# Attention into a mixture of experts: V's split on ScalarE and VectorE, eight weight sums on VectorE, and another order for attention

## The chip, the cores and the metric

One core of a Trainium2 chip runs the whole program in one launch. The engines are TensorE (PE for its matmuls, PEld for its weight loads), VectorE (DVE), ScalarE (ACT), GpSimd (POOL) and SyncE (SP), each with its own queue that runs in program order; engines wait for each other through semaphores. The metric is device time in microseconds (us). Before the change three runs took 1684.28, 1685.58 and 1691.61 us; their median is 1685.58 us.

## The reference

Attention over 4 batches, 8 heads, 576 positions and a head width of 64, with rotary position turns on q and k; its output is the input x (2304 tokens by 512) of a mixture of 8 experts, all of which see all tokens:

```python
q_rot, k_rot = (rotate(q), rotate(k))
scores = 1.0 / np.sqrt(D) * np.matmul(q_rot, k_rot.transpose(0, 1, 3, 2))
attn = np.exp(scores - np.max(scores, axis=-1, keepdims=True))
attn = attn / (np.sum(attn, axis=-1, keepdims=True) + 1e-09)
x = np.matmul(attn, v)                      # tokens by 512
logits = x @ w_gate                         # 8 experts
P = np.exp(logits - logits.max())
for _ in range(8):
    P /= P.sum(1, keepdims=True) + 1e-09
    P /= P.sum(0, keepdims=True) + 1e-09
    P *= N / E
for e in range(E):
    out += P[:, e:e + 1] * (np.maximum(x @ w1[e], 0.0) @ w2[e])
```

## The kernel before

**Number format.** Operands of most matmuls are split into a half-precision high part and a half-precision low part (the rest after the high part is taken away), and three products (high by high, high by low, low by high) are summed. So each operand has an instruction that makes its high part and one that makes its low part. Values are first scaled by a power of two taken from the tensor's largest magnitude.

**Attention.** The work goes by 16 pairs of heads. A pair has five score operations on TensorE (line 406, tile `s`), which make nine units of 128 queries; the third operation makes one unit, the others two. A unit passes VectorE's row maximum (line 410, `nm`), ScalarE's exponential (line 417), VectorE's reciprocal of the row sum (lines 423 and 425), ScalarE's scaled high part (line 428, `et`), VectorE's low part (line 292, `et`) and a DMA transpose from SP's queue (lines 458 and 462, `ET<-et`). When five or four units of a pair are transposed, TensorE multiplies them with V (line 477, `g<-ET,vv`, 30 matmuls for half a pair), and lines 487 and 489 write the high and low part of x (`xx`). Scores lie in three PSUM tiles, so a new score operation waits until an older unit has left its tile. In 4 units of 9 the exponential goes to SBUF (tile `e`), in the other 5 it stays in PSUM (`s`). GpSimd turns q and k of the coming pairs (lines 357 and 361, tile `raw`, six instructions a pair).

**V.** V comes a batch (four pairs) at a time. VectorE takes its largest magnitude (line 289, `vmx`, then `vm`), TensorE and VectorE spread it over the partitions (lines 660, 664, 667), VectorE makes the scale. Then each pair has three steps: `v_x` on GpSimd (line 384) multiplies V by the scale in place, `v_hi` on ScalarE (line 379) rounds it to the high part, `v_lo` on GpSimd (line 388) subtracts.

**Expert 0 as filler.** Expert 0's matmuls F1 (line 611) and F2 (line 630) fill TensorE while attention runs: F1 may begin when the first batch's x and the split of w1 are there, F2 when the split of w2 is there. That split has the same three steps as V's (lines 549, 545, 553, eight of each for w1 and for w2).

**Between attention and the experts** (from about 426 us) TensorE finishes expert 0; VectorE runs the gate's eight normalisations (lines 852 to 864), sums over blocks of x (lines 912 to 937) and the splits of the first half of expert 1's weights (line 292, `w1l` and `w2l`). The later experts use a scheme with seven products in place of eight, for which the weight quarters are added and subtracted four times per matrix; `total` (line 1042) does this on GpSimd, in place, so the order is: split three quarters, four sums, split the four sums. All weights of one matrix lie in one staging tile; the next matrix is loaded when the last split has read it.

**The order.** `Plan.run` lists every operation with an engine, an assumed duration and a due number `at`, and puts them into the engines' queues by a simulated schedule: of the operations that are ready on a free engine, the one with the lowest due number goes first. Durations are in `US`; due numbers are `AT` or `AT_NEW` (by operation, counted in units) plus a shift from `SH1`. GpSimd operations, and VectorE operations marked `lock`, are not planned at the same time. The experts' part has a plan of its own.

Of the kernel before, what the change touches and what calls it, by code (L numbers as in the profile page):

```python
# [14 lines left out]
ALU = mybir.AluOpType  # L15
# [47 lines left out]
    ld=-78.23, cq=-29.0, ck=-28.0, vx=-11.0, sq=-29.0, sk=-28.0, aq=-28.5, ak=-27.5, vh=-10.0, vl=-9.0, h0=4.69, l0=5.19,  # L63
    h1=9.69, l1=10.19, S=-20.0, M=-20.0, ex=-20.0, eh=-10.0, el=-10.0, TR=-10.0, AV=5.0, ei=-20.0,
)
AT_NEW = dict(ldv=-30.41, v0=-10.46, v1=-9.46, v2=-8.46, v3=-7.46, vg=-6.96, vr=-6.86, vp=-6.46)
AV_AT = ((3, 0, 0), (3, 0, 1), (4, 0, 2), (5, 0, 3), (6, 0, 4), (7, 1, 0), (8, 1, 1), (9, 1, 2), (10, 1, 3), (11, 1, 4))

SH1 = dict(
    cq=11.55, sq=11.55, aq=11.55, el=9.37, vh=-16.21, ld=10.14, M=-76.45, S=-26.64, eh=-9.66, ex=-20.25, ck=-11.34,  # L70
    sk=-11.34, ak=-11.34, ldv=-6.42, AV=-36.11, TR=10.32, vx=11.72, vl=-32.41, x0=1.13, h0=1.13, l0=1.13, x1=1.13,
    h1=1.13, l1=1.13, ei=-12.59,
)

US = dict(
# [147 lines left out]
def attention_moe(ctx, tc, qk, v, trigs, eye, wg, w1, w2, out):  # L223
# [67 lines left out]
    def stt_lo(lo, x, s, hi):  # L291
        dve.scalar_tensor_tensor(lo, x, s, hi, op0=ALU.mult, op1=ALU.subtract)  # L292
# [82 lines left out]
    def v_hi(p):  # L375
        t = att.tile([P, 2, 640], F16, tag="vv", bufs=NVV, name="vv")
        vhl[p] = [t[:, n].rearrange("p (j a d) -> p j a d", j=2, a=5) for n in range(2)]
        b, c = divmod(p, KC)
        act.copy(vhl[p][0], vraw[b][:, c])

    def v_x(p, e):
        b, c = divmod(p, KC)
        x = vraw[b][:, c].rearrange("p j a d -> p (j a d)")
        engine[e].tensor_scalar(x, x, vs[b], None, op0=ALU.mult)

    def v_lo(p, e):
        b, c = divmod(p, KC)
        engine[e].tensor_tensor(vhl[p][1], vraw[b][:, c], vhl[p][0], op=ALU.subtract)

    HEADS = [slice(0, 64), slice(64, P)]  # L390
    QH = [slice(0, HS), slice(HS, S)]
# [258 lines left out]
    def choice(pool_us, dve_us):  # L650
        return (("pool", US[pool_us]), ("none", 0.0))[:1] + ((("dve", US[dve_us]),) if BOTH else ())
# [25 lines left out]
    def pair_ops(p):  # L677
# [4 lines left out]
        def add(k, e, us, fn, deps=(), **kw):  # L682
            e = e if isinstance(e, tuple) else (e, US[us])
            plan.add(f"{k}.{p}", e, at[k], fn, [d if "." in d else f"{d}.{p}" for d in deps], **kw)
# [11 lines left out]
        for i in range(5):  # L696
# [14 lines left out]
            for j in range(1 if i == TAIL else 2):  # L711
# [19 lines left out]
                    f"TR.{m}", ("sp", US["TR"]), at["TR"] + u + off(u), lambda m=m: e_turn(m), [f"el.{m}"] + [f"et{h}.{p}" for h in hs],  # L731
                    uses=[e] + [(f"ET{h}", p) for h in hs], allocs=tails if u == 4 else [],
                )
        add("vx", choice("tsv", "tsd"), 0, lambda e: v_x(p, e), [f"vp.{b}"], uses=[("vraw", b)])
        add("vh", "act", "vh", lambda: v_hi(p), ["vx"], allocs=[("vhl", p)], uses=[("vraw", b)])
        add("vl", choice("plv", "tt"), 0, lambda e: v_lo(p, e), ["vh"], uses=[("vraw", b), ("vhl", p)])
        done = None
        for s, qh, jt in AV_AT:
            a, et = ("G", ("av", p, qh)), (f"ET{qh}", p)
# [63 lines left out]
    def w0_ops():  # L803
        plan.add("gx", ("dve", 0.3), 8, gate_max)
        last, g = top_ops("g", 8, "gx", lambda: w0m["g"])
        plan.add("gs", ("dve", 1.0), 8, gate_scale, [last], uses=[g], lock=True)
        for n, at in ((1, 16.95), (2, 66.94)):
            r = ("raw0", n)
            for i in range(4):
                plan.add(  # L810
# [147 lines left out]
    def w_part(plan, q, n, w, at, gap, last):  # L958
# [3 lines left out]
        def put(k, eng, us, fn, deps, **kw):  # L962
            nonlocal at
            at += gap
            plan.add(f"{k}.{n}.{q}", (eng, us), at + (SH2.get(k[0:2], 0.0) if q else 0.0), fn, [x if "." in x else f"{x}.{n}.{q}" for x in deps], **kw)
# [57 lines left out]
        def quad(a, d=d, n=n):  # L1023
            if n == 1:
                x = d["r"].rearrange("p (c h f) -> p c h f", c=KC, h=2)
                return {"11": x[:, 0:2, 0], "12": x[:, 2:4, 0], "21": x[:, 0:2, 1], "22": x[:, 2:4, 1]}[a]
            x = d["r"].rearrange("p (h c e f) -> p h c e f", h=2, c=2, e=2)
            return x[:, int(a[0]) - 1, :, int(a[1]) - 1]
# [10 lines left out]
            put(f"wl{i}", "dve", US["wl"], lambda: lo(i, a), [f"wh{i}"], uses=[raw], lock=True)  # L1039

        def total(k, o, x, y, op, deps):
            put(k, "pool", US["ptt"], lambda: pool.tensor_tensor(quad(o), quad(x), quad(y), op=op), deps, uses=[raw])  # L1042

        if n == 1:
            split(A22, "22")
# [378 lines left out]
```

## Time and profile before

| what | us |
|---|---|
| median of three runs | 1685.58 |
| the profiled execution | 1691.59 |
| its span, first to last instruction | 1689.6 |
| PE busy, 13990 matmuls | 1583.7 |
| DVE busy | 1377.7 |
| ACT busy | 1054.4 |
| POOL busy | 616.1 |

The busy times are of the whole span; two thirds of it is the experts' stage, which keeps TensorE full. The page's 40 slices of 42.2 us show three stages: in the first six TensorE is busy for three to eight tenths, in the next six for nine, and then for nine to the end. The granted TensorE clock is 0.97 on the mean, and below full speed only in slices of attention. The profiled execution took 6.0 us more than the median run, so differences are worked out against it and then taken from the median.

### The profile page before, as it was taken

What the parts mean: (1) busy time and instruction counts of PE and PEld (TensorE: products, weight loads), DVE (VectorE), ACT (ScalarE), POOL (GpSimd) and SP (SyncE); (2) the same over time, 40 slices, a digit from 0 to 9 for tenths busy, and PEclk for the clock granted to TensorE, in tenths of its full rate; (3) what the DMA queues carried; (4) which work ended last, traced back from release to release, by engine and by line L of the source; (5) the groups of instructions that cost most, each with busy time, mean ns of one, the idle gap of its engine ahead of it and who ended that gap; (6) DMA issues with size and microseconds to landing.
All of it is one profiled execution on the core that took longest, in us unless ns stands there. A gap on an engine that the chain in (4) does not pass through costs nothing.

```text
span 1689.6 us, 35290 instructions
## 1 busy us (share of the span) xinstructions
PE 1583.7 (94%) x13990; PEld 1274.3 (75%) x13990; DVE 1377.7 (82%) x2736; ACT 1054.4 (62%) x2145; POOL 616.1 (36%) x504
## 2 busy tenths in 40 slices
PE   3676889999998999999999999999999999999998
PEld 2343445445456898989989898989898989898987
DVE  7667977877797888888888888888888878888877
ACT  3565766656237666666666666666666666666642
POOL 4767774620252423232323323232323323333310
PEclk9767988999999999999999999999999999999999
DMA  7899989977122565656555565655555555565532
GB/s 215 176 184 189 213 177 188 190 155 125 54 88 100 125 151 125 151 132 157 125 151 136 140 138 143 157 131 146 138 151 138 143 133 155 126 161 130 127 111 94
DMA packets 244853, 243.61 MB, mean 144 GB/s; under 512 B 195792, under 2 KB 195920, under 8 KB 241104
## 3 DMA queue, kind: packets, MB, share of 16 engines
q1 hardware_dynamic: 225968, 180.02, 39.5%
q0 software_dynamic: 18720, 61.35, 20.3%
q8 instruction: 109, 1.79, 0.4%
q14 instruction: 56, 0.46, 0.1%
HBM read 123.36 MB, written 9.44 MB: 79 GB/s over the span
## 4 chain that ended last, share of the span: by engine, by line
PE 79%; DVE 8%; DMA 3%; ACT 2%; issue 2%; SPq 0%; POOLq 0%; ACTq 0%; DVEq 0%
PE m L1092 66%; PE s L406 4%; PE g L477 4%; DMA ET<-et 3%; PE g L630 3%; PE g L611 2%; DVE et L292 2%; DVE nm L410 1%; DVE hl L621 1%; DVE ts L912 0%; ACT accA L879 0%; ACT et L428 0%; ACT e L417 0%; DVE w1l L292 0%; DVE ei L425 0%
## 5 line engine op out<-in xcount | busy, mean ns | idle before, releaser
L1092 PE MATMUL m<-w2h,h 128*128 128x256 f16 x3528 | 627.2, 273 | 3.2 <-DVE accB L1155 1.5
L1092 PEld LDWEIGHTS <-h 128*128 128x128 f16 x5292 | 515.3, 98 | 63.5 <-issue 2.0
L1092 PE MATMUL m<-w2l,h 128*128 128x256 f16 x1764 | 480.8, 273 | 0.0
L1092 PEld LDWEIGHTS <-w1h 128*128 128x128 f16 x3920 | 369.2, 98 | 39.9 <-issue 3.0
L1092 PE MATMUL m<-ts,w1h 128*128 128x256 f16 (+1 forms) x2240 | 347.6, 262 | 2.7 <-ACT m L1115 1.4
L1157 ACT ACTIVATE ev<-m,pp 128x256 f32<-128x256 f32 x468 | 197.6, 467 | 185.8 <-PE m L1092 184.8
L1092 PE MATMUL m<-ts,w1l 128*128 128x256 f16 (+1 forms) x1120 | 284.0, 262 | 0.0
L1092 PE MATMUL m<-xx,w1h 128*128 128x256 f16 (+1 forms) x1680 | 261.4, 262 | 0.0
L1042 POOL TENSOR_TENSOR wraw<-wraw 128x512 f32<-128x512 f32 x112 | 160.8, 1436 | 169.3 <-issue 140.6
L1092 PE MATMUL m<-xx,w1l 128*128 128x256 f16 (+1 forms) x840 | 213.1, 262 | 0.0
L1137 POOL TENSOR_TENSOR h<-u,h 128x512 f16<-128x512 f32 (+1 forms) x70 | 78.2, 1116 | 357.7 <-ACT h L1133 348.8
L1092 PEld LDWEIGHTS <-w1l 128*128 128x128 f16 x1960 | 191.8, 98 | 17.7
L1155 DVE SCALAR_TENSOR_TENSOR ev<-m,pp,ev 128x256 f32<-128x256 f32 x351 | 154.8, 478 | 45.4 <-ACT ev L1157 28.3
L406 PE MATMUL s<-raw 64*128 64x288 f32 (+1 forms) x640 | 136.7, 509 | 49.7 <-ACT e L417 19.5
L1133 ACT ACTIVATE h<-m 128x512 f16<-128x512 f32 (+1 forms) x210 | 120.4, 574 | 44.4 <-PE m L1092 40.8
L406 PEld LDWEIGHTS s<-raw 64*128 64x128 f32 (+1 forms) x640 | 72.2, 211 | 99.8 <-issue 28.0
L410 DVE TENSOR_REDUCE nm<-s 128x1 f32<-128x576 f32 x144 | 103.6, 752 | 48.6 <-PE s L406 48.1
L1118 DVE TENSOR_TENSOR u<-m,u 128x512 f32<-128x512 f32 (+1 forms) x140 | 88.9, 635 | 54.9 <-PE m L1092 29.2
L1133 ACT ACTIVATE h<-u 128x512 f16<-128x512 f32 (+1 forms) x210 | 122.4, 586 | 14.8 <-DVE u L1144 11.1
L1115 ACT COPY u<-m 128x512 f32<-128x512 f32 (+1 forms) x140 | 75.8, 541 | 71.5 <-PE m L1092 70.4
L1165 POOL DMA_DIRECT2D accA<-ev x78 | 69.0, 1021 | 126.5 <-ACT ev L1157 108.4
L1165 POOL DMA_DIRECT2D accB<-ev x52 | 45.1, 867 | 181.7 <-ACT h L1133 111.0
(148 smaller groups left out, 2629.8 us busy)
## 6 DMA issues: line engine op xcount, KB each, us to landing
ts<-xd SPq DMA_DIRECT2D x110, 512.0 KB, 3.8
accA<-ev POOLq DMA_DIRECT2D x78, 512.0 KB, 6.1
wraw<-in_w SPq DMA_DIRECT2D x28, 1024.0 KB, 4.9
raw<-in_qk SPq DMA_DIRECT2D x32, 576.0 KB, 5.0
accB<-ev POOLq DMA_DIRECT2D x26, 512.0 KB, 7.1
ts<-xd SPq DMA_DIRECT2D x28, 256.0 KB, 2.9
accB<-ev POOLq DMA_DIRECT2D x26, 256.0 KB, 3.3
vraw<-in_v SPq DMA_DIRECT2D x16, 320.0 KB, 4.4
```

Of the source, the lines that this page charges most:

```text
L406: pe.matmul(o, q, x[r, 1, QH[kh]], start=True, stop=True)
L410: dve.tensor_reduce(b[0], ps[:, :, 0:HS], axis=AX.XY, op=ALU.max, negate=True)
L477: pe.matmul(po[r, m : m + e.shape[-1]], x[:, j, jt, :], e[:, j, 5 * n + jt, :], start=jt == i == 0 and x is vh and n == 0, stop=jt == 4 an ...
L1042: put(k, "pool", US["ptt"], lambda: pool.tensor_tensor(quad(o), quad(x), quad(y), op=op), deps, uses=[raw])
L1092: pe.matmul(live[bank][:, f_ * width : (f_ + 1) * width], step(x, i, f_), y[:, i], start=first and f_ == 0 and n == 0, stop=n == 5, skip_g ...
L1115: act.copy(live[n], live[src])
L1118: dve.tensor_tensor(live[n], live[x], live[n], **add)
L1133: act.activation(t[:, 0:cols], live[src], func)
L1137: engine[eng].tensor_tensor(l, live[src], h, **sub)
L1155: dve.scalar_tensor_tensor(o, x, s, o, op0=ALU.mult, op1=ALU.add)
L1157: act.activation(o, x, AF.Copy, scale=s)
L1165: pool.dma_start(out=accs(th * NT2 + t0_, nt), in_=ev[th][:, 0:nt], accum_op=ALU.add)
```

## The change

V's split loses the step `v_x`: `v_hi` now scales and rounds in one ScalarE instruction (`hi_of`), and `v_lo` scales and subtracts in one VectorE instruction (`stt_lo`, a scalar_tensor_tensor on V, the scale and the high part). 32 GpSimd instructions go, 16 VectorE instructions come. In the first half-expert after expert 0 (`q == 0`) the eight sums of weight quarters go from GpSimd to VectorE. The shifts `SH1`, V's due numbers and those of expert 0's weights are other numbers, and the queues of the attention stage come out in another order. The helpers `hi_of` and `stt_lo` are those that the later experts' weights use already.

```diff
--- before.py
+++ after.py
@@ -63,13 +63,13 @@
...
 )
-AT_NEW = dict(ldv=-30.41, v0=-10.46, v1=-9.46, v2=-8.46, v3=-7.46, vg=-6.96, vr=-6.86, vp=-6.46)
+AT_NEW = dict(ldv=-30.41, v0=-13.01, v1=-12.01, v2=-11.01, v3=-10.01, vg=-9.51, vr=-9.41, vp=-9.01)
 AV_AT = ((3, 0, 0), (3, 0, 1), (4, 0, 2), (5, 0, 3), (6, 0, 4), (7, 1, 0), (8, 1, 1), (9, 1, 2), (10, 1, 3), (11, 1, 4))
 
 SH1 = dict(
-    cq=11.55, sq=11.55, aq=11.55, el=9.37, vh=-16.21, ld=10.14, M=-76.45, S=-26.64, eh=-9.66, ex=-20.25, ck=-11.34,
...
+    cq=-13.64, sq=-13.64, aq=-13.64, el=6.36, vh=-33.79, ld=6.54, M=-83.95, S=-86.81, eh=-10.31, ex=-37.95, ck=7.42,
...
 )
 
 US = dict(
@@ -376,16 +376,11 @@
         t = att.tile([P, 2, 640], F16, tag="vv", bufs=NVV, name="vv")
         vhl[p] = [t[:, n].rearrange("p (j a d) -> p j a d", j=2, a=5) for n in range(2)]
         b, c = divmod(p, KC)
-        act.copy(vhl[p][0], vraw[b][:, c])
-
-    def v_x(p, e):
+        hi_of(vhl[p][0], vraw[b][:, c], vs[b])
+
+    def v_lo(p):
         b, c = divmod(p, KC)
-        x = vraw[b][:, c].rearrange("p j a d -> p (j a d)")
-        engine[e].tensor_scalar(x, x, vs[b], None, op0=ALU.mult)
-
-    def v_lo(p, e):
-        b, c = divmod(p, KC)
-        engine[e].tensor_tensor(vhl[p][1], vraw[b][:, c], vhl[p][0], op=ALU.subtract)
+        stt_lo(vhl[p][1], vraw[b][:, c], vs[b], vhl[p][0])
 
     HEADS = [slice(0, 64), slice(64, P)]
     QH = [slice(0, HS), slice(HS, S)]
@@ -731,9 +726,8 @@
                     f"TR.{m}", ("sp", US["TR"]), at["TR"] + u + off(u), lambda m=m: e_turn(m), [f"el.{m}"] + [f"et{h}.{p}" for h in hs],
                     uses=[e] + [(f"ET{h}", p) for h in hs], allocs=tails if u == 4 else [],
                 )
-        add("vx", choice("tsv", "tsd"), 0, lambda e: v_x(p, e), [f"vp.{b}"], uses=[("vraw", b)])
-        add("vh", "act", "vh", lambda: v_hi(p), ["vx"], allocs=[("vhl", p)], uses=[("vraw", b)])
-        add("vl", choice("plv", "tt"), 0, lambda e: v_lo(p, e), ["vh"], uses=[("vraw", b), ("vhl", p)])
+        add("vh", "act", "vh", lambda: v_hi(p), [f"vp.{b}"], allocs=[("vhl", p)], uses=[("vraw", b)])
+        add("vl", "dve", "vl", lambda: v_lo(p), ["vh"], uses=[("vraw", b), ("vhl", p)], lock=True)
         done = None
         for s, qh, jt in AV_AT:
             a, et = ("G", ("av", p, qh)), (f"ET{qh}", p)
@@ -804,7 +798,7 @@
         plan.add("gx", ("dve", 0.3), 8, gate_max)
         last, g = top_ops("g", 8, "gx", lambda: w0m["g"])
         plan.add("gs", ("dve", 1.0), 8, gate_scale, [last], uses=[g], lock=True)
-        for n, at in ((1, 16.95), (2, 66.94)):
+        for n, at in ((1, 16.2), (2, 104.48)):
             r = ("raw0", n)
             for i in range(4):
                 plan.add(
@@ -1039,7 +1033,8 @@
             put(f"wl{i}", "dve", US["wl"], lambda: lo(i, a), [f"wh{i}"], uses=[raw], lock=True)
 
         def total(k, o, x, y, op, deps):
-            put(k, "pool", US["ptt"], lambda: pool.tensor_tensor(quad(o), quad(x), quad(y), op=op), deps, uses=[raw])
+            e_ = "dve" if q == 0 else "pool"
+            put(k, e_, US["tt" if q == 0 else "ptt"], lambda: engine[e_].tensor_tensor(quad(o), quad(x), quad(y), op=op), deps, uses=[raw], lock=True)
 
         if n == 1:
             split(A22, "22")
```

The first place is VectorE at the beginning, some 35 us into the run: `vm` is V's maximum for the first batch, `wgs` the gate's weights, `wmx` the maximum of expert 0's weights, `top` the step that spreads a maximum. Before:

```order
L279 TENSOR_SCALAR e<-g 128x1
L283 TENSOR_SCALAR inv<-e 128x1
L285 RECIPROCAL s<-inv 128x1
L588 TENSOR_SCALAR wgs<-wgt,s 128x4x8
L589 SCALAR_TENSOR_TENSOR wgs<-wgt,s,wgs 128x4x8
L289 TENSOR_REDUCE wmx<-wraw 128x1
L289 TENSOR_REDUCE vmx<-vraw 128x1
L328 TENSOR_REDUCE vm_299<-vmx 128x1
L289 TENSOR_REDUCE wmx<-wraw 128x1
L664 TENSOR_REDUCE top_309<-g 1x1
```

Now:

```order
L289 TENSOR_REDUCE wmx<-wraw 128x1
L289 TENSOR_REDUCE vmx<-vraw 128x1
L328 TENSOR_REDUCE vm_297<-vmx 128x1
L292 SCALAR_TENSOR_TENSOR et_99<-s,ei,et_99 128x576
L659 TENSOR_REDUCE top_311<-g 1x1
```

The gate's scale and split (lines 279 to 589 of before) stood ahead of the last part of V's maximum; now they come after the first two low parts of V, 24 rows of the order later than V's maximum. On TensorE the turn of this maximum stood with its second matmul directly ahead of the scores of the second pair; now a score operation of four matmuls lies between the two matmuls.

The second place is GpSimd from the third pair's turns on: `raw` with `trig` and `trigq` are k's and q's turns, `vraw` and `vv` V, `wraw` and `wl` expert 0's weights. Before:

```order
L357 TENSOR_TENSOR raw<-raw,trig 128x576 x2
L361 TENSOR_TENSOR raw<-raw 128x576
L357 TENSOR_TENSOR raw<-raw,trigq 128x576 x2
L384 TENSOR_SCALAR vraw<-vraw,s 128x640
L361 TENSOR_TENSOR raw<-raw 128x576
L384 TENSOR_SCALAR vraw<-vraw,s 128x640
L388 TENSOR_TENSOR vv<-vraw,vv 128x640 x2
L357 TENSOR_TENSOR raw<-raw,trig 128x576 x2
L361 TENSOR_TENSOR raw<-raw 128x576
L357 TENSOR_TENSOR raw<-raw,trigq 128x576 x2
L361 TENSOR_TENSOR raw<-raw 128x576
L384 TENSOR_SCALAR vraw<-vraw,s 128x640 x2
```

Now:

```order
L357 TENSOR_TENSOR raw<-raw,trigq 128x576 x2
L361 TENSOR_TENSOR raw<-raw 128x576
L357 TENSOR_TENSOR raw<-raw,trig 128x576 x2
L361 TENSOR_TENSOR raw<-raw 128x576
L357 TENSOR_TENSOR raw<-raw,trigq 128x576 x2
L361 TENSOR_TENSOR raw<-raw 128x576
L357 TENSOR_TENSOR raw<-raw,trig 128x576 x2
L361 TENSOR_TENSOR raw<-raw 128x576
L544 TENSOR_SCALAR wraw<-wraw,s 128x512 x2
L548 TENSOR_TENSOR wl<-wraw,wh 128x512
L544 TENSOR_SCALAR wraw<-wraw,s 128x512
```

V's steps are gone from between the turns, and expert 0's first weight split follows the turns directly. In the whole stage the last low part of w1 now stands after the turns of 5 pairs, where it stood after 6; the last of w2 after those of 10, where it stood after 9 (pair 0's turns, which `prep0` makes, are not counted). On TensorE the first F1 matmul comes after 24 of the 80 score operations and before after 28; the first F2 after 46 and before after 41. By the 46th score operation 96 of the 480 filler matmuls of attention had been placed, and before 132. F1 and F2 of the same blocks are left for after attention in both. The multiplications with V of the first two pairs come one to three score operations sooner, most others stand as far behind their scores as before.

The third place is VectorE in the stage between attention and the experts, from the last gate operation on (line 866 of before, 860 now); 1037 is `total`. Before:

```order
L866 TENSOR_TENSOR prob<-prob,ctok 128x144
L292 SCALAR_TENSOR_TENSOR w1l<-wraw,s,w1h 128x512
L925 TENSOR_TENSOR m_5083<-m_5083,c_5084 128x512
L927 TENSOR_TENSOR u_5085<-xx,m_5083 128x512
L292 SCALAR_TENSOR_TENSOR w1l<-wraw,s,w1h 128x512
L930 TENSOR_TENSOR u_5085<-u_5085,xx 128x512
L912 TENSOR_TENSOR ts<-m_5083,ts 128x512
L933 TENSOR_TENSOR u_5086<-xx,u_5085 128x512
L292 SCALAR_TENSOR_TENSOR w1l<-wraw,s,w1h 128x512
L937 TENSOR_TENSOR u_5086<-u_5086,xx 128x512
L912 TENSOR_TENSOR ts<-u_5085,ts 128x512
L912 TENSOR_TENSOR ts<-u_5086,ts 128x512
```

Now:

```order
L860 TENSOR_TENSOR prob<-prob,ctok 128x144
L1037 TENSOR_TENSOR wraw<-wraw 128x2x256
L919 TENSOR_TENSOR m_5059<-m_5059,c_5060 128x512
L921 TENSOR_TENSOR u_5061<-xx,m_5059 128x512
L1037 TENSOR_TENSOR wraw<-wraw 128x2x256
L924 TENSOR_TENSOR u_5061<-u_5061,xx 128x512
L906 TENSOR_TENSOR ts<-m_5059,ts 128x512
L927 TENSOR_TENSOR u_5062<-xx,u_5061 128x512
L1037 TENSOR_TENSOR wraw<-wraw 128x2x256
L931 TENSOR_TENSOR u_5062<-u_5062,xx 128x512
L906 TENSOR_TENSOR ts<-u_5061,ts 128x512
L292 SCALAR_TENSOR_TENSOR w1l<-wraw,s,w1h 128x512
```

Four sums (three of them in these rows) stand where low parts of sums stood, and those low parts come later, among the sums over x; so the staging tile of the weights comes free later, and the next matrix's load stands on SP behind two more stores of x's sums. The experts' own part has the same instructions in the same order on TensorE, VectorE and ScalarE.

## Rows read from the trace of the kernel before

**Rows 1.** Stretches: length; busy PE, PEld, DVE, ACT, POOL (instructions); granted clock; DMA share; GB/s.
```profile
42.00:252.00 210.00, 157.13 (x996) 88.77 (x994) 158.55 (x351) 134.04 (x283) 155.64 (x105) 0.80 0.91 187
252.00:426.00 174.00, 161.98 (x1272) 87.56 (x1270) 130.60 (x295) 112.03 (x232) 59.01 (x40) 0.96 0.84 162
426.00:521.40 95.40, 90.32 (x510) 46.35 (x510) 85.31 (x162) 33.92 (x63) 42.59 (x32) 1.00 0.21 76
...
545.00:1689.60 1144.60, 1138.98 (x11002) 1027.00 (x11002) 960.01 (x1843) 735.04 (x1495) 338.28 (x303) 1.00 0.54 137
```

**Rows 2.** The same view for line 410 alone, VectorE busy (x units).
```profile
42.00:252.00 210.00, 53.31 (x74) 0.80 0.91 187
```

**Rows 3.** Chain of waits, 84 to 130 and 225 to 262 us: start, length, what.
```profile
101.25 2.27 PE s L406 x8
...
114.54 3.73 PE g L477 x30
118.27 1.22 PE s L406 x8
...
236.19 3.99 PE g L630 x18
...
241.35 1.96 PE g L477 x30
```

**Rows 4.** Chain of waits, 0 to 426 us, shares by line.
```profile
by line: PE s L406 14.6%; PE g L477 14.5%; DMA ET<-et 13.4%; PE g L611 7.4%; DVE et L292 6.4%; PE g L630 6.2%; DVE nm L410 5.7%; issue 3.3%; ACT et L428 1.2%; ACT e L417 1.0%; DVE ei L425 0.9%; DVE xx L489 0.9%; DVE vmx L289 0.9%; DVE hl L6
```

**Rows 5.** GpSimd, 0 to 426 us, by line and shape: busy, mean ns.
```profile
L384 POOL TENSOR_SCALAR vraw<-vraw,s 128x640 f32<-128x640 f32 x16 | 31.5, 1975 | 2.0 <-DVE s L285 2.0
...
L388 POOL TENSOR_TENSOR vv<-vraw,vv 128x640 f16<-128x640 f32 x16 | 22.4, 1397 | 68.8 <-ACT vv L379 68.8
```

**Rows 6.** VectorE, 0 to 426 us: line 292 (min/median/max ns), then two groups.
```profile
L292 DVE SCALAR_TENSOR_TENSOR et<-s,ei,et x80: 796/809/819, 20.0 to 414.3; 128x576 f16<-128x576 f32 x80
L292 DVE SCALAR_TENSOR_TENSOR et<-e,ei,et x64: 796/819/1982, 28.5 to 413.3; 128x576 f16<-128x576 f32 x64
...
L292 DVE SCALAR_TENSOR_TENSOR et<-e,ei,et 128x576 f16<-128x576 f32 x64 | 66.1, 1032 | 0.9 <-ACT et L428 0.8
...
L289 DVE TENSOR_REDUCE vmx<-vraw 128x1 f32<-128x640 f32 x16 | 12.9, 806 | 0.0
```

**Rows 7.** ScalarE by line and shape, whole span.
```profile
L296 ACT ACTIVATE w1h<-wraw,s 128x512 f16<-128x512 f32 x98 | 66.5, 714 | 4.0 <-POOL wraw L1042 3.6
...
L545 ACT CAST wh<-wraw 128x512 f16<-128x512 f32 x16 | 9.4, 625 | 0.0
```

**Rows 8.** Waits, 0 to 426 us: total us, times, longest.
```profile
PE s L406 <- DVE et L292: 15.4, 10, 4.9
...
PE s L406 <- POOL vv L388: 1.8, 1, 1.8
```

**Rows 9.** Timeline, 34.5 to 41.2 us: start, length, engine, line, idle before.
```profile
35.41 0.56 DVE L588 TENSOR_SCALAR wgs<-wgt,s 128x32 f16<-128x32 f32 x1
36.01 1.45 DVE L589 SCALAR_TENSOR_TENSOR wgs<-wgt,s,wgs 128x32 f16<-128x32 f32 x1
...
39.56 0.27 PE L660 MATMUL g<-idt,vm 128*1 128x128 bf16 x1 [8.72 <-DVE vm L328]
```

**Rows 10.** Stretches of 42 us (columns as in Rows 1).
```profile
126.00:168.00 42.00, 28.42 (x215) 16.32 (x210) 31.23 (x68) 24.41 (x53) 30.19 (x20) 0.80 1.00 195
210.00:252.00 42.00, 36.04 (x217) 19.84 (x218) 30.54 (x75) 28.59 (x62) 32.31 (x23) 0.79 0.87 177
```

**Rows 11.** 426 to 521.4 us: VectorE sums of the same shape, GpSimd weight sums.
```profile
L930 DVE TENSOR_TENSOR u<-u,xx 128x512 f32<-128x512 f32 x4 | 4.6, 1158 | 0.1
...
L937 DVE TENSOR_TENSOR u<-u,xx 128x512 f32<-128x512 f32 x4 | 2.7, 682 | 0.0
...
L1042 POOL TENSOR_TENSOR wraw<-wraw 128x512 f32<-128x512 f32 x8 | 12.2, 1528 | 19.5 <-DVE w2l L292 8.7 <-DVE w1l L292 6.9 <-issue 3.9
```

**Rows 12.** Timeline of VectorE at 528 us (columns as in Rows 9).
```profile
528.07 0.69 DVE L1118 TENSOR_TENSOR m<-m,m 128x512 f32<-128x512 f32 x1 [6.50 <-ACT m L1115]
```

More of the change, by code (lines that the diff above doesn't have):

```diff
@@ L65 @@
 )
-AT_NEW = dict(ldv=-30.41, v0=-10.46, v1=-9.46, v2=-8.46, v3=-7.46, vg=-6.96, vr=-6.86, vp=-6.46)
+AT_NEW = dict(ldv=-30.41, v0=-13.01, v1=-12.01, v2=-11.01, v3=-10.01, vg=-9.51, vr=-9.41, vp=-9.01)
 AV_AT = ((3, 0, 0), (3, 0, 1), (4, 0, 2), (5, 0, 3), (6, 0, 4), (7, 1, 0), (8, 1, 1), (9, 1, 2), (10, 1, 3), (11, 1, 4))
 SH1 = dict(
-    cq=11.55, sq=11.55, aq=11.55, el=9.37, vh=-16.21, ld=10.14, M=-76.45, S=-26.64, eh=-9.66, ex=-20.25, ck=-11.34,
-    sk=-11.34, ak=-11.34, ldv=-6.42, AV=-36.11, TR=10.32, vx=11.72, vl=-32.41, x0=1.13, h0=1.13, l0=1.13, x1=1.13,
-    h1=1.13, l1=1.13, ei=-12.59,
+    cq=-13.64, sq=-13.64, aq=-13.64, el=6.36, vh=-33.79, ld=6.54, M=-83.95, S=-86.81, eh=-10.31, ex=-37.95, ck=7.42,
+    sk=7.42, ak=7.42, ldv=-8.03, AV=-24.8, TR=54.89, vx=28.87, vl=-16.76, x0=-4.1, h0=-4.1, l0=-4.1, x1=-4.1,
+    h1=-4.1, l1=-4.1, ei=8.29,
 )
```

## The prediction

> **What bounds the kernel now.** I read first the busy time by stretch [rows 1]. From 545 us on TensorE is busy for 1138.98 of 1144.60 us, and the instructions there are the same in the same order: nothing to gain or lose. From 426 to 521.4 us TensorE is busy for 90.32 of 95.40 us and VectorE for 85.31, so the stage belongs to TensorE, with 10.1 us of slack on VectorE. Attention is in two parts. From 252 to 426 us TensorE is busy for 161.98 of 174 us. From 42 to 252 us it is busy for 157.13 of 210 us, at a granted clock of 0.80; VectorE has 158.55 us, GpSimd 155.64 us, ScalarE less, and no engine is full. There 74 units pass [rows 2], 2.84 us each, or 5.1 us for each score operation (144 units in 80 operations).
>
> Second, the chain of waits. In the first 426 us it goes through TensorE (scores 14.6%, V 14.5%), the transposes (13.4%) and VectorE's reductions and low parts (5.7% and 6.4%); GpSimd is not among the lines that it names [rows 4]. So the first half is a ring (scores, maximum, exponential, low part, transposes, scores) in which each engine's delay counts for a part. TensorE's part depends on its clock: eight score matmuls take 2.27 us at one place and 1.22 us at another, a V block of 30 takes 3.73 us and later 1.96 us [rows 3]; the two levels are 1.2 and 2.4 GHz. Third, the waits: TensorE waited 15.4 us for low parts before scores and 1.8 us for GpSimd's V step [rows 8].
>
> **The change part by part.**
>
> V off GpSimd: 16 x 1.975 + 16 x 1.397 = 54.0 us go [rows 5], of the 215 us that GpSimd is busy from 42 to 426 us (155.64 and 59.01 [rows 1]). Of this only the 1.8 us that TensorE waited for V stands on the path: -1.8 us, bounds 0 and -5.
>
> V's low part on VectorE: the trace has no such instruction on 640 columns; the nearest is the unit's low part on 576. Its median is 0.819 us, its mean with both inputs in SBUF 1.032 us, its longest 1.982 us [rows 6]. Scaled by 640/576 the clean one is 0.91 us. The mean lies 0.213 us above the median; with GpSimd's work down to 161 of 215 us I take 0.16 us of that for all such instructions. So V's 16 cost 16 x 1.07 = 17.1 us, and the 64 units' low parts get back 64 x 0.05 = 3.2 us: VectorE +13.9 us. How much of this is on the path? The reduction over V, also 16 instructions of 0.8 us put between the units, is busy for 12.9 us and has 0.9% of the chain's 426 us, 3.8 us, which is 30% [rows 4, 6]; the 144 row maxima (53.31/74 = 0.72 us each [rows 2], 5.7%, 24 of 104 us) give 23%. At 25%: +3.5 us. Bounds: 0 if all lies in VectorE's idle time, and 16 x 1.98 - 3.2 = +28.5 us if every one is held up and every one is on the path; I stay near the reduction's row.
>
> The unit's low part with one input in PSUM never took more than 0.819 us, with two in SBUF up to 1.982 us [rows 6]. By the Trainium skill ("SBUF — State Buffer", Who interferes with whom) a VectorE instruction with two SBUF inputs and a GpSimd instruction that reads SBUF shut each other out for the whole of an instruction; the trace agrees. That speaks against this change, since V's new low part reads both its tensors from SBUF: it doesn't leave the shared port, it only holds it for a shorter time.
>
> V's high part: ScalarE's plain copy of 512 columns takes 0.625 us, the scaled one 0.714 us [rows 7]; 0.089 x 640/512 x 16 = 1.8 us on an engine whose two lines have 2.2% of the chain [rows 4]: +0.1 us.
>
> The beginning: at 35.41 us the gate's scaling and split (0.56 and 1.45 us, to 37.46) stand on VectorE ahead of V's maximum, for which TensorE waited 8.72 us with the second pair's scores behind it [rows 9]. They are moved behind: -2.0 us. Bounds 0 (then V's load is late) and -8.7.
>
> Filler: F1 begins 3.5 score operations sooner on the mean (24 to 25 for 28), 18 us, in a stretch where TensorE was idle for 32% (28.42 busy of 42): 5.8 us of matmuls find idle time. F2 begins five operations later, 25.5 us, where it was idle for 14% (36.04 of 42): 3.6 us of idle time go unused [rows 10]. Together -2.2 us. Bounds: for a gain, all of the 15.4 us before scores [rows 8]; for a loss, the 36 filler matmuls that no longer stand in the first 46 operations, 36 x 3.99/18 = 8.0 us [rows 3], put into the part where TensorE has 7% idle [rows 1]. The rest of the new order (score and V blocks mostly as far apart as before) I count as nothing, because the same 2.84 us per unit rule it.
>
> Weight sums: eight sums cost VectorE 0.682 to 1.158 us each, 5.5 to 9.3 us, by the block sums of the same shape without and with GpSimd beside them; GpSimd loses 12.2 of 42.6 us [rows 1, 11]. The four group means above 0.682 us in that view come mostly from GpSimd, so VectorE gets some of it back, and 10.1 us of slack covers the rest. The second matrix's load starts some 4 to 7 us later (the last low part of the first matrix comes behind six more block sums), covered too, since VectorE stood idle for 6.50 us ahead of the first expert block [rows 12]. 0 us, bounds -3 and +4; if the cover is gone, the first expert block waits.
>
> Sum: -1.8 + 3.5 + 0.1 - 2.0 - 2.2 + 0 = -2.4 us. The profiled execution took 1691.59 us, so it would take 1689.2; it is 6.0 us above the median run, and against the median of 1685.58 us I predict **1683.2 us**. No change is what a measurement can't tell from 0.5%, 8.4 us.
>
> **The rivals.**
>
> A, the beginning opens up: 1673 us. If V's maximum was late only through VectorE's queue, the whole 8.72 us goes, and the early F1 fills idle time with nothing given back (5.8 us); with the VectorE and GpSimd terms (+3.5, -1.8) -12.8 us. For it: the last of V's reductions stood behind 2.0 us of gate work and a weight maximum. Against it: V's fourth part is loaded behind transposes, and the order of the loads is nearly the same. It decides if the second pair's scores begin near 32 us instead of 41.
>
> B, TensorE gets slow in the middle: 1698 us. Between the 33rd and the 46th score operation no filler stands, where before the gap went from the 36th to the 41st. The stretches around such gaps ran at 0.79 and 0.80 [rows 10]. Eight operations more at the low level, of which each costs 0.53 us more, are 4.2 us; three V blocks at 1.77 us more are 5.3 us [rows 3]. The 8.0 us of filler are then missing and fall into the nearly full part; with +3.5 us of VectorE, -2.0 at the beginning and -1.8 of GpSimd the sum is +17.2 us, of which a quarter (TensorE's idle share from 42 to 252 us [rows 1]) hides: +12.9. It decides if the granted clock from 200 to 260 us stays at 0.8 or falls under it, and F2 is late at 426 us.
> The clock was at the lower level for part of a stretch in which TensorE was idle for 32% and of one in which it was idle for 14% [rows 10]. By the Trainium skill ("TensorE: Matmul & The Clock Gate", Part 1) low speed is the state that the engine falls back to and activity ends it; here that makes idle stretches dear, which is this rival.
>
> C, the port gives nothing back: 1688 us. V's low part is held up by a whole GpSimd instruction as often as not, 1.5 us each, 16 x 0.91 + 16 x 0.75 = 26.6 us, at 25% +6.6, less 1.8 and 2.0, and the filler even: +2.8. This is also the case in which the change does no more than move work from one waiting engine to another.
>
> **How the numbers follow.** The forecast (attention within a few us, 1676 to 1690) has 0.43, A 0.27, B 0.21, C 0.09. Faster by over 0.5% (under 1677.2): A but for a little, and a sixth of the forecast, 0.33. Slower by over 0.5% (over 1694.0): four fifths of B and some of the forecast and of C, 0.20. Within: 0.47. The range that leaves out a tenth at each end goes to 1665 (A with half of the 15.4 us on top) and to 1700 (B with most of C's 2.8 us).
>
> **What would show it.** V's low part on VectorE at 0.9 to 1.2 us; GpSimd 54 us less before attention's end and 12 us less after it; the last unit's transposes at 415 to 425 us of the span; TensorE's first wait for V's maximum at 5 to 7 us; some 95 us from attention's end to the first expert matmul, as now. The forecast is wrong if the second pair's scores begin before 35 us (A), if the stretch between 200 and 260 us has a lower clock and fewer units (B), or if the stage after attention grows by more than 4 us, which no case here has.

## The result and the profile after

The changed kernel takes **1669.86 us** (median of 4 runs, 1669.00 to 1672.45) against 1688.59 us of the kernel before in the same session (4 runs, 1684.28 to 1691.75): ratio 0.9887, 95% interval 0.9863 to 0.9912. It is 1.1% faster. The time lies in the range of the prediction, but its likeliest case, no change, is not what came: the case that did was "faster by over 0.5%", with 0.33.

Stretches of the changed kernel, cut at its own attention's end (last V matmuls at 404.8 us) and first expert matmul; columns as in [rows 1]:
```profile
42.00:252.00 210.00, 164.17 (x1100) 96.29 (x1098) 173.45 (x393) 143.55 (x301) 124.91 (x86) 0.81 0.97 199
252.00:404.80 152.80, 146.31 (x1159) 77.48 (x1158) 119.86 (x270) 103.23 (x212) 36.72 (x25) 1.00 0.87 167
404.80:499.70 94.90, 90.30 (x509) 46.26 (x508) 82.97 (x170) 33.95 (x65) 28.95 (x24) 1.00 0.22 80
523.40:1667.20 1143.80, 1138.52 (x10999) 1026.52 (x10997) 958.77 (x1842) 734.36 (x1495) 338.36 (x303) 1.00 0.54 137
```
Attention ends at 404.8 instead of 426 us. The stage behind it takes 94.9 us for 95.4, the experts the same as before. So the whole gain is inside attention. From 42 us to attention's end TensorE is now busy for 310.5 of 362.8 us, before for 319.1 of 384: it stands idle for 52.3 us, before for 64.9.

The profile of before is of a run of 1691.59 us, 3 us over its median. The experiment with the sums alone has the instructions of before in the same order up to attention's end; its profile, cut at its own end:
```profile
42.00:252.00 210.00, 157.48 (x1027) 88.69 (x1027) 160.23 (x355) 135.58 (x283) 157.70 (x107) 0.83 0.91 189
252.00:418.40 166.40, 153.60 (x1234) 82.46 (x1235) 127.84 (x290) 109.99 (x229) 55.13 (x38) 0.99 0.87 165
```
By this profile the gain in attention is 13.6 us, by the one of before 21.2; the medians say 18.7. The two profiles of the old attention share their idle time, 65.3 and 64.9 us, 13.0 and 12.6 more than now. Their busy time differs by 8.0 us at a different granted clock (0.83 and 0.99, before 0.80 and 0.96 [rows 1]).

The line of the row maxima alone, which answers to [rows 2], 77 units for 74 (73 with the sums alone):
```profile
42.00:252.00 210.00, 55.22 (x77) 0.81 0.97 199
```
And all engines in stretches of 42 us, of which the first and the last answer to [rows 10]:
```profile
126.00:168.00 42.00, 38.95 (x277) 20.42 (x275) 35.60 (x79) 27.94 (x58) 13.63 (x10) 0.96 1.04 207
168.00:210.00 42.00, 30.72 (x175) 16.96 (x175) 33.20 (x78) 28.63 (x59) 27.53 (x20) 0.76 0.89 194
210.00:252.00 42.00, 36.04 (x270) 22.00 (x268) 34.79 (x81) 29.86 (x63) 25.59 (x18) 0.79 0.91 172
```
From 126 to 168 us TensorE is busy for 38.95 us at a granted clock of 0.96, where it was busy for 28.42 at 0.80 [rows 10]. Of that, its score matmuls are 64 in 14.15 us before and 70 in 11.32 us after (rows at the experiment on F1): 221 and 162 ns each. The next stretch goes the other way, 0.76 now and 0.96 before:
```profile
168.00:210.00 42.00, 34.67 (x237) 18.03 (x237) 38.70 (x81) 30.51 (x65) 30.96 (x22) 0.96 0.89 207
```
There 72 score matmuls take 18.41 us now, and 66 took 10.79 us before.

The operations of the sum. VectorE's low parts (min/median/max ns, first and last start), as in [rows 6]; the third is V's new one:
```profile
L292 DVE SCALAR_TENSOR_TENSOR et<-s,ei,et x80: 795/808/819, 19.2 to 393.2; 128x576 f16<-128x576 f32 x80
L292 DVE SCALAR_TENSOR_TENSOR et<-e,ei,et x64: 797/810/2046, 27.4 to 392.5; 128x576 f16<-128x576 f32 x64
L292 DVE SCALAR_TENSOR_TENSOR vv<-vraw,s,vv x16: 865/876/1384, 44.5 to 360.8; 128x640 f16<-128x640 f32 x16
```
ScalarE's scaled V copy up to 405 us (busy, mean ns, idle before), which answers to [rows 7]:
```profile
L296 ACT ACTIVATE vv<-vraw,s 128x640 f16<-128x640 f32 x16 | 12.9, 820 | 7.8 <-PE g L472 7.7
```
GpSimd up to 405 us has no line of V any more, for [rows 5]; the line with the longest idle time before it is a rotary product:
```profile
L357 POOL TENSOR_TENSOR raw<-raw,trigq 128x576 f32<-128x576 f32 x30 | 44.6, 1493 | 109.9 <-DMA raw<-in_qk 103.6 <-DVE gm L289 4.5 <-PE g L662 1.6
```
VectorE from 404.8 to 499.7 us with the weight sums that GpSimd had in [rows 11]:
```profile
L1037 DVE TENSOR_TENSOR wraw<-wraw 128x512 f32<-128x512 f32 x8 | 5.5, 686 | 0.1
```
In front of the rotary line GpSimd stands idle for 103.6 us until queries and keys are loaded. The timeline at the start, first of VectorE, as in [rows 9]:
```profile
36.55 0.16 DVE L328 TENSOR_REDUCE vm<-vmx 128x1 bf16<-128x4 f32 x1
```
and then of TensorE:
```profile
36.77 0.27 PE L655 MATMUL g<-idt,vm 128*1 128x128 bf16 x1 [4.24 <-DVE vm L328]
36.96 3.23 PE L401 MATMUL s<-raw 64*128 64x288 f32 x8
```
The wait for V's maximum fell from 8.72 to 4.24 us, the second pair's scores start at 36.96 us instead of 40.97. With the sums alone, in the old order, the wait was 7.63 us and the start 39.09, so the order itself accounts for 2.1 of the 4.0 us.

The lead grows before there is filler to speak of. The 25th score operation (eight matmuls each; start and length), in the kernel before and in the changed one, where F1 has just begun:
```profile
142.11 1.24 PE L406 MATMUL s<-raw 64*128 64x288 f32 x8
130.40 1.24 PE L401 MATMUL s<-raw 64*128 64x288 f32 x8
```
Two more profiles of the old order have it at 138.10 (the sums alone) and 135.86 us (F2 held), two of the new order at 131.40 (the sums back on GpSimd) and 128.78 us (F1 held). So the new order is some 4 to 13 us ahead there. TensorE's waits up to 410 us, as in [rows 8]:
```profile
PE g L472 <- DMA ET<-et: 25.7, 22, 3.5
PE s L401 <- ACT e L412: 12.7, 12, 2.6
...
PE s L401 <- DVE et L292: 9.7, 9, 1.6
PE g L655 <- DVE vm L328: 6.0, 2, 4.2
```

### The profile page after: what moved, and what is told of

The parts are those of the page before. It is cut to its first block, busy times and chain, and to the rows that moved or that the text cites. A ratio compares the mean times of both kernels' runs of the same rounds, so it can differ in the third digit from the quotient of the medians.

```text
span 1667.2 us, 35270 instructions
## 1 busy us (share of the span) xinstructions
PE 1579.8 (95%) x13990; PEld 1273.4 (76%) x13990; DVE 1379.1 (83%) x2760; ACT 1055.4 (63%) x2145; POOL 550.9 (33%) x464
## 4 chain that ended last, share of the span: by engine, by line
PE 78%; DVE 6%; DMA 2%; ACT 2%; issue 1%; SPq 0%; POOLq 0%; ACTq 0%; DVEq 0%
PE m L1087 67%; PE g L625 3%; PE g L472 2%; PE g L606 2%; PE s L401 2%; DMA ET<-et 2%; DVE et L292 1%; DVE nm L405 1%; DVE ts L906 1%; ACT accA L873 0%; DVE hl L616 0%; DVE w1l L292 0%; DVE wmx L289 0%; DVE u L931 0%; DMA vraw<-in_v 0%
## 5 line engine op out<-in xcount | busy, mean ns | idle before, releaser
L1037 POOL TENSOR_TENSOR wraw<-wraw 128x512 f32<-128x512 f32 x104 | 148.6, 1429 | 150.0 <-issue 137.1
L472 PE MATMUL g<-ET,vv 128*64 128x288 f16 (+1 forms) x960 | 87.4, 329 | 28.0 <-DMA ET<-et 25.7
```

What stands on the lines that cost most here:

```text
L472: pe.matmul(po[r, m : m + e.shape[-1]], x[:, j, jt, :], e[:, j, 5 * n + jt, :], start=jt == i == 0 and x is vh and n == 0, stop=jt == 4 an ...
L1037: put(k, e_, US["tt" if q == 0 else "ptt"], lambda: engine[e_].tensor_tensor(quad(o), quad(x), quad(y), op=op), deps, uses=[raw], lock=True)
```

## The experiments

Names: "tables" are the offsets SH1 and AT_NEW and the two times of the expert weights. F1 and F2 are the filler; "left" counts the filler matmuls that stand behind the last score operation in TensorE's order. The median of before was 1689.1 to 1689.7 us in these sessions.

| run | median us | ratio (95%) | F1 / F2 start behind score op. | left | attention's end | first expert | span |
|---|---|---|---|---|---|---|---|
| before | 1688.59 | 1 | 28 / 41 | 474 | 425.7 | 521.3 | 1689.6 |
| changed | 1669.86 | 0.9887 (0.9863-0.9912) | 24 / 46 | 480 | 404.5 | 499.7 | 1667.2 |
| V alone | 1686.72 | 0.9988 (0.9978-0.9999) | 26 / 44 | 444 | 418.1 | 515.1 | 1682.6 |
| tables alone | 1725.65 | 1.0206 (1.0184-1.0229) | 31 / 60 | 615 | 415.4 | 546.4 | 1714.7 |
| changed, sums on GpSimd | 1670.22 | 0.9896 (0.9879-0.9912) | 24 / 46 | 480 | 407.8 | 504.2 | 1671.7 |
| sums alone | 1686.12 | 0.9986 (0.9972-1.0000) | 28 / 41 | 474 | 418.1 | 512.5 | 1680.8 |
| new order, old V split | 1674.34 | 0.9912 (0.9896-0.9927) | 24 / 46 | 480 | 412.0 | 507.2 | 1674.7 |
| new order, V scaled on GpSimd | 1674.47 | 0.9918 (0.9903-0.9934) | 24 / 46 | 480 | 408.1 | 503.3 | 1670.8 |
| V + sums | 1683.95 | 0.9969 (0.9956-0.9982) | 26 / 44 | 444 | 422.2 | 511.3 | 1683.9 |
| V + SH1 + sums | 1681.84 | 0.9959 (0.9944-0.9974) | 26 / 40 | 408 | 421.8 | 502.7 | 1683.7 |
| the same, F2 held | 1678.76 | 0.9930 (0.9916-0.9943) | 26 / 47 | 498 | 415.1 | 514.6 | 1682.9 |
| before, F2 held | 1700.39 | 1.0058 (1.0044-1.0073) | 28 / 47 | 492 | 422.3 | 523.9 | 1692.2 |
| V + SH1, no sums | 1678.84 | 0.9938 (0.9926-0.9950) | 26 / 40 | 408 | 418.6 | 498.7 | 1676.7 |
| changed, F1 held | 1679.97 | 0.9947 (0.9930-0.9964) | 30 / 47 | 474 | 414.7 | 509.9 | 1677.4 |

The last three columns are from the one profile of each (last start of a V matmul, first start of an expert matmul). The profiled run can lie off the median: 1716.80 us with the tables alone, 1685.52 with V + SH1 + sums, 1684.75 with F2 held there, 1694.46 with F2 held in before.

**V alone.** V's edit of the diff (scaled copy and GpSimd's low part out, `hi_of` and `stt_lo` in), nothing else.

> Only V's split is changed (no scaled copy, ScalarE writes the high part with the scale, VectorE the low part); the tables of times and the weight sums are those of before. Theory Q (the gain is GpSimd's queue: V's two steps stood there behind ScalarE and held up the transposed gate and weight steps behind them): most of the 18.7 us, so 1670 to 1676 us, attention's end at 405 to 411 us, the first weight's last low part on GpSimd near 110 us and the first F1 near 130 us. Theory O (the refitted tables give it): under 6 us, 1683 to 1689 us. The forecast's own sum for this part alone (-1.8 + 3.5 + 0.1): 1690 us.

1686.72 us, 2 us faster. Theory Q falls: with GpSimd's V steps gone, first F1 is at 146.4 us and little is won. (The planner lays the work anew here too, F1 behind the 26th and F2 behind the 44th operation, so the run is not the price of V's steps alone.) But TensorE's filler ended at 506.2 us, and then it stood. Its timeline there (start, length, line, tiles, idle before):
```profile
506.15 0.38 PE L625 MATMUL g<-wh,hl 128*128 128x512 f16 x1
...
515.13 0.58 PE L1086 MATMUL m<-xx,w1h 128*128 128x256 f16 x2 [8.59 <-ACT accB L630]
```
ScalarE, which has to copy F2's results out, was late. So having less filler left behind attention was no use: something else needed 97.0 us from attention's end.

**The tables alone.** SH1, AT_NEW and `((1, 16.2), (2, 104.48))` put into the kernel before.

> The tables of times of the changed kernel, with V's split and the weight sums of before. Theory Q: no gain, 1686 to 1695 us, and V's steps on GpSimd still wait 2 to 5 us each for ScalarE; tables fitted to another set of instructions can even lose. Theory O: 1670 to 1676 us. What both can show: the first wait for V's maximum falls from 8.7 to about 4 us here, since this comes from the tables.

1725.65 us, 2% slower, outside both. The planner lays the work anew around the numbers: with V still on GpSimd it lets F1 and F2 begin behind the 31st and the 60th score operation, and 615 filler matmuls are left. TensorE's F1 and F2 groups (count, min/median/max ns, first and last start):
```profile
L611 PE MATMUL g<-xx,wh x320: 322/379/390, 160.6 to 530.5; 128*128 128x512 f16 x96, 128*128 128x384 f16 x64
...
L630 PE MATMUL g<-wh,hh x144: 376/379/634, 305.5 to 545.7; 128*128 128x512 f16 x144
```
The tables are no change of their own; they are a fit to one set of instructions. What was expected under both theories came: the first wait for V's maximum is 4.25 us. In this form the run tells nothing on theory O, which needs the order itself.

**The sums.** Back to GpSimd in the changed kernel (`e_ = "pool"`), and alone in the kernel before.

> The changed kernel with the first expert's weight sums back on GpSimd. Forecast: 0 us against the changed kernel, 1670 us, bounds 1666 to 1673. The stage from attention's end to the first expert matmul 94 to 97 us. The rival that the sums carry a part of the gain: 1674 us or more.

> The kernel before with only the first expert's first weight sums moved to VectorE. Forecast: 0 us, 1685 to 1691 us; the stage after attention stays at 95 us within 2. Rival: GpSimd was late in that stage, and the stage gets shorter by 3 to 6 us.

Nothing (1670.22 for 1669.86), and at most 0.3% (1686.12). As forecast.

**The new order with V's old split.** Every instruction stays where the changed kernel has it, but
```
-        hi_of(vhl[p][0], vraw[b][:, c], vs[b])
+        pool.tensor_scalar(x, x, vs[b], None, op0=ALU.mult)
+        act.copy(vhl[p][0], vraw[b][:, c])
...
-        stt_lo(vhl[p][1], vraw[b][:, c], vs[b], vhl[p][0])
+        pool.tensor_tensor(vhl[p][1], vraw[b][:, c], vhl[p][0], op=ALU.subtract)
```


> The changed kernel with every instruction in its place, but V's split done as before: the scaled copy and the low part on GpSimd, put exactly where the changed kernel has ScalarE's high part and VectorE's low part; 16 instructions leave VectorE, 32 come to GpSimd. Unlike the order alone (1725.65 us), the filler keeps its places here. Theory Q (GpSimd must be free of V for the gain): the weight's low parts and the turned queries and keys come late again, attention's end at 415 to 430 us instead of 404.5, time 1682 to 1700 us. Theory O (the order alone is what pays): 1668 to 1675 us, attention's end at 403 to 409 us.

> As the run before, but only the scaled copy of V stays on GpSimd (16 x 1.975 = 31.6 us, which wait for no ScalarE step); the low part is on VectorE, a plain subtraction. If Q holds by waiting (GpSimd standing behind ScalarE): near the changed kernel, 1670 to 1676 us. If Q holds by occupancy: about 60% of what the run with both steps loses (31.6 of 54.0 us). Theory O: 1668 to 1675 us.

1674.34 and 1674.47 us, both in theory O's range; in the second run VectorE's low part is a plain subtraction. Theory O holds, Q falls: 15 of the 19 us are there with V on GpSimd as before, though attention's end, 412.0 us in the first run, lies between O's range and Q's. TensorE's waits of the first of the two:
```profile
PE s L403 <- DVE et L292: 12.9, 12, 1.9
...
PE g L474 <- POOL vv L385: 2.0, 1, 2.0
```
It waits 2.0 us for GpSimd's V step and 3.2 us more for low parts than the changed kernel. V's move is worth some 4.5 us in this order (the intervals just overlap), and the scaled copy alone, which waits for no ScalarE step, costs as much as both steps: so it is not the standing behind ScalarE.

**V and the sums, then with SH1.**

> V's split and the weight sums as changed, the tables of times of before. In the run with V's split alone the filler ended at 506.2 us but the first expert matmul started at 515.1, 97.0 us after attention's end, behind ScalarE; with the sums on VectorE this stage took 93.2 to 95 us to the last low part. So 2 to 4 us under that run: 1682 to 1685 us. If the tables have no part in the gain: 1670 to 1674 us.

> As the run before, and the large table of offsets of the changed kernel; V's own loads and maxima keep their times of before. If that table carries the rest: 1668 to 1676 us and attention's end at 403 to 409 us. If it needs the 2.55 units' earlier V maxima too: 1678 us or more.

1683.95 and 1681.84 us. The first is as expected; the large table adds little, and the rest, 12 us, comes only with AT_NEW (the two times of the expert weights change no engine's order, with either AT_NEW). With SH1 alone the planner puts more filler into attention: 408 matmuls are left, TensorE is through with them 79.6 us after attention's end, begins the first expert, and stands there:
```profile
PE m L1087 <- ACT m L1110: 11.4, 1, 11.4
```
From attention's end to the end of the span it takes 1261.9 us, in the changed kernel 1262.7, with V alone 1264.5, before 1263.9. Whoever ends the filler sooner gets nothing for it.

**Leaving out the sums there.** `lambda: q and ...`: the eight sums of the first expert's first weights are not made.

> The run with V's split, the large table and the sums (1681.84 us), in which TensorE began the first expert 80.9 us after attention's end and then stood 13 us; here the eight sums of the first expert's first weights are left out, 5.5 us of VectorE behind attention. Theory D (VectorE is the floor of that stage, 83 us busy of 94): 4 to 6 us less, 1676 to 1678 us. The premise of the forecast (VectorE has 10 us of slack there, the stage is TensorE's): 0, 1680 to 1684 us.

1678.84 us, 3.0 less by the medians (the intervals of the two ratios overlap), and 1258.1 us from attention's end, 3.8 less; the wait is shorter:
```profile
PE m L1087 <- ACT m L1110: 6.5, 1, 6.5
```
Of 5.5 us of VectorE 3 to 4 come out, just under the 4 to 6 us of theory D and off the 0 of the forecast's premise. So where TensorE is through with its filler early, VectorE's work sets the length of this stage, nearly in full. Whether by its load or because the sums stand ahead of the splits of the same weights, the run does not separate.

**F2 held.** One more dependency on the first F2 matmul, `["S.46.0"] if k == 0`.

> The run with V's split, the large table and the sums (1681.84 us), with one more condition: the first F2 matmul stands behind the 46th score operation, where the changed kernel has it, instead of the 40th. 498 filler matmuls are then left for the time after attention, against 408 there and 480 in the changed kernel. Theory F (the gain is the balance of filler before and behind attention's end: the time is attention's end plus some 1262 us, and filler done inside attention delays that end): 90 x 0.22 = 19.8 us earlier at most, so attention's end at 402 to 410 us and 1667 to 1674 us. Theory R (the changed kernel's ring of scores, maxima and low parts is itself faster, by V's earlier maxima): attention's end stays over 415 us, 1678 us or more.

> The kernel before with the same one condition (first F2 behind the 46th score operation, not the 41st): 492 filler matmuls left instead of 474. Theory F: before was already in balance (474 against the 480 of the changed kernel), so at most 18 x 0.22 = 4 us, 1684 to 1689 us. Theory R: no change at all within 0.3%. If the place of F2 by itself were the cure: 1675 us or less.

1678.76 us and attention's end at 415.1 us, just inside theory R's ranges. But attention's end does come earlier, by 6.7 us for 90 matmuls moved behind it, not the 20 of theory F. And the kernel before gets **slower**, 1700.39 us, which neither theory had. The stretch from 210 to 252 us, without F2 in it, all engines, in the kernel before with F2 held:
```profile
210.00:252.00 42.00, 27.97 (x191) 18.48 (x192) 31.38 (x73) 25.51 (x56) 32.41 (x22) 0.63 0.87 179
```
and in the kernel with V's split, SH1 and the sums, with F2 held:
```profile
210.00:252.00 42.00, 34.49 (x246) 21.65 (x244) 33.82 (x82) 28.64 (x63) 16.01 (x12) 0.75 0.94 193
```
With F2 the old order has 36.04 us busy at 0.79 there [rows 10], and 35.96 at 0.84 in the profile with the sums alone. So in the kernel before TensorE has 8 us less to do there, stands idle for 14.0 us and not for 6.0, and the clock falls to 0.63. Over attention (from 42 us) it is idle for 69.0 us, 4 more than in the two profiles without the condition. From attention's end, 422.3 us, to the first expert matmul it takes 101.6 us, for 95.6 in before, with 18 more filler matmuls left, 4 us of work. So the loss is some 4 us inside attention and 6 behind it. Theory F falls as it stood: taking filler out of the first half does not pull attention's end forward by its length. (The profiled run took 1694.46 us, the median is 1700.39; where those 6 us lie it does not show.)

**F1 held in the changed kernel.** The same kind of condition on the first F1 matmul (`["S.28.0"]`) and on F2. The order comes out with F1 behind the 30th operation and F2 behind the 47th; up to the first F1 matmul of the changed kernel, at 127.7 us, it is the same.

> The changed kernel with two conditions: the first F1 matmul stands behind the 28th score operation, as in the kernel before, instead of the 24th, and the first F2 stays behind the 46th. The planner orders the rest around this; 474 filler matmuls are left for the time after attention, as in the kernel before. Theory G (in the changed kernel the early first batch gives TensorE filler from 128 us on, and the stretch from 126 to 168 us then runs at 0.96 and not at 0.80; all runs with F1 at 128 to 131 us ended attention by 412 us, all others after it): attention's end at 413 to 421 us, the stretch at 0.85 or less, 1678 to 1688 us. Theory R (V's earlier maxima and the rest of the tables make the ring faster, filler or not): attention's end at 404 to 410 us, 1668 to 1674 us.

1679.97 us, attention's end at 414.7 us and the stretch at 0.80, all as theory G expected. 10.1 of the 18.7 us are gone with F1's early place. The stretch from 126 to 168 us, all engines:
```profile
126.00:168.00 42.00, 28.22 (x206) 16.26 (x202) 33.58 (x77) 26.77 (x56) 19.56 (x14) 0.80 0.95 202
```
and its score matmuls alone (busy PE, PEld; granted clock):
```profile
126.00:168.00 42.00, 16.03 (x70) 8.09 (x66) 0.80 0.95 202
```
The same row of the changed kernel:
```profile
126.00:168.00 42.00, 11.32 (x70) 6.08 (x68) 0.96 1.04 207
```
and of the kernel before:
```profile
126.00:168.00 42.00, 14.15 (x64) 7.35 (x64) 0.80 1.00 195
```
With 12 filler matmuls in the stretch 70 score matmuls take 16.03 us, with 84 of them 11.32. That looks like the cause: filler makes its neighbours fast. But the next stretch gives it back. The same row from 168 to 210 us, with F1 held and in the changed kernel:
```profile
168.00:210.00 42.00, 11.57 (x64) 6.20 (x64) 0.96 0.86 177
168.00:210.00 42.00, 18.41 (x72) 9.13 (x72) 0.76 0.89 194
```
and from 42 us to the last score operation, in the same order:
```profile
42.00:430.00 388.00, 117.60 (x591) 61.03 (x590) 0.89 0.88 177
42.00:430.00 388.00, 116.18 (x590) 59.71 (x588) 0.90 0.88 178
```
All score matmuls together differ by 1.4 us. What differs is idle time. All engines with F1 held, cut at attention's end:
```profile
42.00:252.00 210.00, 156.04 (x1028) 91.57 (x1027) 169.87 (x379) 137.81 (x289) 125.79 (x86) 0.80 0.93 194
252.00:414.90 162.90, 155.24 (x1232) 81.75 (x1231) 126.80 (x285) 109.09 (x224) 35.47 (x25) 1.00 0.86 164
```
TensorE is busy for 311.3 us and idle for 61.6, in the changed kernel busy for 310.5 and idle for 52.3. (The other profile of the changed kernel's attention, with the sums back on GpSimd, has 309.6 and 56.4.) So 9.3 of the 10.1 us between the two ends are idle time of TensorE that the early F1 fills, by the other profile 5.2 of 6.9. Theory R is not refuted for the other half: with F1 held the kernel still beats before by 9.4 us, and its 25th score operation begins at 128.78 us, as early as in the changed kernel. The planner also moves other work around such a condition, and no run had the ring of the changed kernel with filler exactly as before.

## Why the prediction was right and wrong

- **What was mis-sized** is the filler term, and the sentence behind it that counts the rest of the new order as nothing "because the same 2.84 us per unit rule it". The filler term was of the right kind: matmuls that find or miss idle time. But it let F1 begin 18 us sooner, by the number of score operations; in time F1 began 24 to 28 us sooner (127.7 us for 151.6 and 155.6), because the ring itself was ahead. At the 32% of idle time that the forecast took from [rows 10] that is 8 to 9 us and not 5.8, and 5 to 9 us of idle time is what the early place filled by the traces. F2 began 11 to 15 us later and not 25.5, and the idle time from 210 to 252 us stayed at 6.0. In the kernel before F2's six later operations cost 0.58%, some 10 us, but of these only 4 are idle time in attention, as the forecast's 3.6.
- **The rest of the new order was not nothing.** The 25th score operation came some 4 to 13 us sooner, of which 2 are from the start; 77 units passed from 42 to 252 us instead of 74 or 73, and 75 still with F1 held. The pace per unit was no constant. What sets it in the new order no run took apart. The kernel with F1 held is 9.4 us faster than before.
- **Rival A** gave 1673, close to the result, by another road: its deciding sign, second scores near 32 us, did not come (36.96), and two thirds of its 12.8 us were to come from the start. So its time is luck. That the early F1 fills idle time is the part of it that held; "with nothing given back" did not, for the next stretch has 11.3 us of idle time and with F1 held 5.4.
- **Rival B** was right as a mechanism and wrong in place. The stretch from 168 to 210 us did fall, from 0.96 to 0.76, and the kernel before with F2 alone held, slower by 0.58%, had 0.63 from 210 to 252 us; in the changed kernel the early F1 more than pays it. (Its sum prices eight score operations at 0.53 us; by [rows 3] eight matmuls, one operation, cost 1.05 us more, so 8.4 us and not 4.2.) By the Trainium skill ("TensorE: Matmul & The Clock Gate", Part 1) the low speed is the resting state and activity ends it; the trace agrees, 0.80 and 0.96 in the same stretch without and with filler.
- **The start**: -2.0 forecast; at the second pair's scores -4.0 by the profile of before, -2.1 by the one with the sums alone. The gate's 2.01 us no longer stand ahead of V's last reduction, as forecast. The other 1.9 us are a difference between two profiles of the old order, no part of the change.
- **V off GpSimd, on VectorE**: -1.8 + 3.5 + 0.1 = +1.8 forecast; about -2 measured alone (with the planner's own new order in it), and some -4.5 in the new order. V's low part takes 0.907 us (14.5/16) and not 1.07, the unit's low parts with both inputs in SBUF fell from a mean of 1032 to 956 ns, 4.9 us for 64 where I took back 3.2. The term was off by 4 to 6 us. The Trainium skill's rule that two-input VectorE work and GpSimd's reads shut each other out ("SBUF — State Buffer", Who interferes with whom) is seen only in the tail here: V's longest is 1.384 us, its median 0.876. GpSimd is busy for 124.9 us from 42 to 252 us, before for 155.6; whether that is why, no run shows. Rival C, with 1.66 us for each, falls.
- **V's high part**: 0.820 us each, for 0.714 x 1.25 = 0.89 by the forecast's row: as small as it was taken.
- **Sums**: 0 forecast, 0 measured. But the reason given, 10.1 us of slack on VectorE in a stage that "belongs to TensorE", was wrong. Attention's end to the span's end is 1261.7 to 1264.5 us in ten profiles with 408 to 480 filler matmuls left, and only over that (492, 498, 615) is it longer: 1269.9, 1267.8 and 1299.3. Before and after the change both bounds meet within a microsecond or two, which looked like one.
- **The expert weights' times** have no effect: with SH1 and AT_NEW in place they change no engine's order.

What stays open: how AT_NEW's 2.55 units (V's maxima earlier) bring first logits from 134.6 to 126.9 us and F1 from 141.2 to 127.7, and which wait gives the ring its lead before there is filler. That the gain is the planner's answer to both tables and V's edit together is shown, and that about half of it hangs on F1's place; a single cause behind the other half is not.

## What to carry to other kernels

A table of due times fitted to one set of instructions is not a part of a change that can be priced alone: put into the kernel before it cost 2%, with V's edit it gave 1%. Price filler by the time by which its start moves, the ring's own lead included, and by the idle time that it finds there. A stretch in which its neighbours run faster is no gain until the whole stage is summed: here the next stretch gave it back, and the idle time of the stage told what was won. And where a stage has one engine at 95% and another at 89%, take both as bounds until a run with one of them relieved says otherwise.

## What the runs showed of the hardware

TensorE with less to do was slower at the rest. With F2 held out of the stretch from 210 to 252 us in the kernel before, its busy time fell from 36.04 us (35.96 in the other profile of that order) to 27.97, and the granted clock from 0.79 (0.84) to 0.63, a mean over the two levels of 1.2 and 2.4 GHz; a score matmul there took 264 ns, for 209 (198). With F1 in the stretch from 126 to 168 us 70 score matmuls took 11.32 us for 16.03, but in the next stretch, now with little filler, 72 took 18.41 us where 64 had taken 11.57: the slow stretch lay elsewhere, and over attention the score matmuls took 116.18 us for 117.60. Filler did not settle it alone: V + SH1 + sums was busy for 37.00 us from 126 to 168 us, 40 filler matmuls among it, at 0.79.

The same instructions in the same order ran attention in 418.1 and 425.7 us: TensorE was idle for 65.3 and 64.9 us, and busy for 311.1 and 319.1, at a granted clock of 0.83 and 0.80 in the first stretch. A single profile of such a kernel is good to some 8 us.
